# Linear attention with a learned feature map: the half-filled product of K, Q and V, for both branches in the two halves of TensorE's rows

## The chip, the cores and the metric

The kernel runs on one core of a Trainium2 chip, in one launch. The metric is the device time of that launch in microseconds. Five engines take part: TensorE (PE in the profile, PEld for its loads of stationary operands), VectorE (DVE), ScalarE (ACT), GpSimdE (POOL) and SyncE (SP), which issues nearly all transfers.

## The reference

Two attention branches, A and B, read the same input of 2048 tokens with 448 channels; each has 16 heads of 28 channels. A sigmoid gate mixes their outputs.

```
def _A_ref(x, wqkv, w_phi, wo):
    B, S, D = x.shape
    H = 16; Dh = D // H
    ...
    q, k, v = qkv[0], qkv[1], qkv[2]
    pq = jnp.einsum("bhsd,hdf->bhsf", q, w_phi)
    pk = jnp.einsum("bhsd,hdf->bhsf", k, w_phi)
    phi_q = jnp.concatenate([_softmax(pq, axis=-1), _softmax(-pq, axis=-1)], axis=-1)
    phi_k = jnp.concatenate([_softmax(pk, axis=-1), _softmax(-pk, axis=-1)], axis=-1)
    kv = jnp.einsum("bhsf,bhsd->bhfd", phi_k, v)
    z  = jnp.einsum("bhsf->bhf", phi_k)
    num = jnp.einsum("bhqf,bhfd->bhqd", phi_q, kv)
    den = jnp.einsum("bhqf,bhf->bhq", phi_q, z)[..., None] + 1e-6
    o = num / den
    return (lambda x, *d: x.transpose(*d))(o, 0, 2, 1, 3).reshape(B, S, D) @ wo
...
g = _sigmoid((x * gate_w).sum(-1, keepdims=True))
return g * a + (1 - g) * b
```

All data are float32.

## The kernel before, in words

**Tiles and products.** The 2048 tokens are 16 tiles of 128. For each tile TensorE makes K, Q and V of both branches (the learned map w_phi is folded into the weights of K and Q ahead, in fold). The matmuls take operands of the type fp32r; to come near float32, each factor is split into a high part and a low part (the rest), and three of the four products are made: high x high, high x low, low x high. The 448 channels are three and a half chunks of 128. The host appends the last 64 channels a second time, so that the fourth chunk has 128 rows: in x its rows 0 to 63 are the high part of these channels, and its rows 64 to 127 are overwritten with their low part (split_x), while the weights hold the same 64 rows twice. One matmul of the fourth chunk with the high weights thus makes two terms at once. With the low weights only its first 64 rows make a wanted term; the product of the low rows with the low weights comes along. The list XT (L414) names the 11 matmuls of a bank: four with the high weights, four with the low ones, and three with the low parts of x. The last of the second four, (3, 1, 3), is the half-filled one. mms (L416) issues them; k_proj, q_proj and v_proj call it once for each branch, with 432, 432 and 450 (branch 0, the gate's column among them) or 448 columns.

**PSUM banks.** K0 and K1 for K of the two branches, Q with two banks, VA and VB for V of the two branches, T0 for the sum over keys, O0 for a product of the last stage.

**What follows a product.** k_soft copies K out of its banks with ACT (pk) and makes its states, the two softmaxes, with reductions on DVE (L486, L487, L493), differences and products on POOL, exponentials on ACT; they lie in one of NE = 3 buffers (ret). v_out copies V with ACT into one of NV = 5 buffers (vs) and the gate's column into glog. q_front reduces Q on DVE (qmx, L520), subtracts into ru and sends it through DRAM (qd) to regroup it; q_soft reads it back and makes its softmaxes; DVE turns the result (L551). Results of tiles 0 to 7 are stored to DRAM (spill) and fetched again at the end. kv_acc (L497, matmuls at L505, T in the profile) adds two tiles' states times V into T0.

**The end.** num multiplies Q's states with the sums (N in the profile, L588, 32x32 tiles), DVE turns the bank (L599), POOL divides and gates, o_turn turns the result and splits it, and out_mm multiplies it with wo (O, 21 matmuls each tile, L636).

**Order.** The work of each step is given to a small planner (class Plan) with an engine, an estimated cost, and what it reads and writes. TensorE's steps run in the order in which steps() yields them; on each other engine the planner simulates the time and takes, of the steps that are ready, the one that is due first. The order that results is fixed at build time, and each engine runs it strictly in that order. The loop over p = 2 to 6 is a round of two tiles each: K of tile 2p, Q of tile 2p-2, kv_acc of 2p-2 and 2p-1, V of 2p+2, then K of 2p+1, Q of 2p-1, V of 2p+3. The inputs x of three pairs of tiles are held (NX = 3): load_x fetches, split_x converts with ACT and subtracts with POOL. In each round one or two chunks of wo are split too (ACT, POOL, and three transfers).

Of the kernel before, what the change touches and what calls it, by code (L numbers as in the profile page):

```python
# [13 lines left out]
P = 128  # L14
# [94 lines left out]
def steps():  # L109
# [5 lines left out]
    for p in range(2, 7):  # L115
        yield "x", p + 1
        yield "K", 2 * p
        yield "Q", 2 * p - 2
        if 2 * p - 2 < JIT:
            yield "S", 2 * p - 2, (JIT - 2 * p + 2) % 3 - 1  # L120
        yield "kv", 2 * p - 2, 2 * p - 1
        yield "wo", p - 2
        if p == 3:
            yield "wo", 6
        if p < 6:
            yield "V", 2 * p + 2
        yield "K", 2 * p + 1
        yield "Q", 2 * p - 1
        if 2 * p - 1 < JIT:
            yield "S", 2 * p - 1, (JIT - 2 * p + 1) % 3 - 1  # L130
        if p < 6:
            yield "V", 2 * p + 3
        if p == 6:
            yield "gates", 0, 12
            yield "gates_b", 0, 12
# [31 lines left out]
def hedgehog_mix(ctx: ExitStack, tc: tile.TileContext, xd, wv, wkt, wqt, wphi, wo, cmask, cpmask, out):  # L167
# [18 lines left out]
    rq = sb.tile([P, 2, 8 * FW], F32R, name="rq")  # L186
    rx = sb.tile([P, NX, 14 * P], F32R, name="rx")
    ret = sb.tile([P, 3 * 2048 + NE * 4 * D], F32, name="ret")
# [32 lines left out]
    wvh, wvl = (rv[:, i].rearrange("p (c n) -> p c n", c=4) for i in range(2))  # L221
    xs = [rx[:, i].rearrange("p (k t) -> p k t", k=7) for i in range(NX)]
    es = [re[:, i].rearrange("p (s n) -> p s n", s=2) for i in range(NE)]
# [15 lines left out]
    def free_v():  # L239
# [5 lines left out]
        mid["oT", 0], mid["oT", 1] = f[:, 6784:7168], ref[:, 4992:5376]  # L245
    hls = [rx[:, i].rearrange("p (s k t) -> p s k t", s=2, k=7) for i in range(NX)]
    obs = [ref[:, 4096 + D * i:4096 + D * i + D] for i in range(2)]
# [17 lines left out]
    def act(o, i, f=AF.Copy, **k):  # L265
        return lambda: A.activation(val(o), val(i), f, **k)  # L266
# [148 lines left out]

    def mms(t, w, name, k, lo, hi):  # L416
        x, o = xs[t // 2 % NX], t % 2 * P
        def go():
            for i, (xc, l, c) in enumerate(XT):
                nc.tensor.matmul(bank[name][:, k, lo:hi], x[:, xc, o:o + P], w[l][:, c], start=i == 0, stop=i == len(XT) - 1)  # L420
# [35 lines left out]

    def v_proj(t, b):
        w, n = v_weights(b)
        n_, k, kb = v_bank(t, b)
        add("PE", 11 * 0.203, mms(t, w, n_, k, 0, n),  # L460
            xkeys(t) + [("v" + h, c, b) for h in "hl" for c in range(4)], [kb])
# [8 lines left out]

    def k_proj(t, b):
        add("PE", 11 * 0.197, mms(t, feat((wkh, wkl), b), f"K{b}", 0, FO, FZ),
            xkeys(t) + wkeys("k", (b,)), [("K", b)])
# [36 lines left out]

    def q_proj(t, b):
        add("PE", 11 * 0.197, mms(t, feat((wqh, wql), b), "Q", b, FO, FZ),
            xkeys(t) + wkeys("q", (b,)), ["Q"])
# [186 lines left out]
    for what, *a in steps():  # L700
# [18 lines left out]
        elif what == "qf":  # L719
            q_front(*a)  # L720
        elif what == "Q":
            for b in range(2):
# [103 lines left out]
```

## Time and profile before

| | us |
|---|---|
| time, median of 3 runs | 338.06 (337.44 to 338.69) |
| the profiled execution's own time | 338.86 |
| its span, first to last instruction | 337.0 |
| PE busy | 329.7 |
| weight loads (PEld) busy | 295.5 |
| DVE busy | 280.6 |
| POOL busy | 250.8 |
| ACT busy | 145.2 |

Busy times are sums over the span; matmuls are pipelined, so that PE counts as busy also where it does not run at its peak. A matmul's record is longer than the distance to the next one's start: 359 ns on the average for Q, of which 352 take 72.1 us together. A row of a group of instructions has the line, the engine, the operation, the tiles written and read, the shapes, the count, the busy time and the mean duration in ns, and then the idle time of the engine before them with what ended it. A row of the timeline has start, length, engine, line, operation, tiles, shapes and count. The chain is followed back from the last instruction, at each step to what released it.

### The profile page before, as it was taken

To read this page: it belongs to the slowest core of one execution; us is meant where nothing else is said; L and a number is where in the kernel's file an instruction comes from. 1 tells how busy PE (TensorE), PEld (TensorE's weight loads), DVE (VectorE), ACT (ScalarE), POOL (GpSimd) and SP (SyncE) were. 2 spreads that over 40 slices of the span, in tenths; PEclk is the share of its full clock that TensorE was granted. 3 is DMA by queue.
4 is the path that set the end of the run, shared out by engine and by line. 5 is a ranking of instruction groups with operands and counts; after the bars stand their busy time and mean duration, and the time that the engine had idled before them with its cause. 6 is when DMAs were issued, how large, how long until landed. Compare 5 with 4: busy or idle time off the path is not lost.

```text
span 337.0 us, 8897 instructions
## 1 busy us (share of the span) xinstructions
PE 329.7 (98%) x3742; PEld 295.5 (88%) x3742; DVE 280.6 (83%) x339; ACT 145.2 (43%) x236; POOL 250.8 (74%) x210
## 2 busy tenths in 40 slices
PE   7999999999999999999999999999999999999994
PEld 6977899998999999999999999999788888788894
DVE  3648879699797896969899979797899999999960
ACT  3747944372365462624445344432052433523331
POOL 7018669999999969989896999694269768887400
PEclk9999999999999999999999999999999999999999
DMA  7773046531297757647646330765886355131011
GB/s 248 215 244 97 2 125 189 165 119 41 70 336 251 217 187 191 238 136 238 217 123 262 88 110 15 277 255 182 236 255 236 135 191 197 61 147 56 31 54 55
DMA packets 29871, 54.73 MB, mean 162 GB/s; under 512 B 4632, under 2 KB 25480, under 8 KB 27528
## 3 DMA queue, kind: packets, MB, share of 16 engines
q1 hardware_dynamic: 29576, 54.06, 48.7%
q8 instruction: 29, 0.48, 0.6%
q0 software_dynamic: 256, 0.12, 0.1%
q14 instruction: 10, 0.08, 0.1%
HBM read 31.54 MB, written 24.22 MB: 165 GB/s over the span
## 4 chain that ended last, share of the span: by engine, by line
PE 65%; DVE 18%; POOL 8%; DMA 4%; issue 3%; ACT 1%; SPq 1%; DVEq 0%; POOLq 0%; ACTq 0%
PE Q L420 15%; PE K L420 14%; PE O L636 10%; PE VA L420 8%; PE VB L420 8%; POOL ret L263 3%; PE T L505 3%; DVE rv L599 3%; POOL rv L608 3%; DVE ret L551 3%; PE N L588 2%; DMA ret<-in_wv 2%; DVE sm L493 2%; DVE rx L263 1%; DVE qsm L546 1%
## 5 line engine op out<-in xcount | busy, mean ns | idle before, releaser
L420 PE MATMUL Q<-rq,rx 128*128 128x432 f32 x352 | 72.1, 359 | 0.0
L420 PE MATMUL K<-rk,rx 128*128 128x432 f32 x352 | 71.8, 359 | 0.0
L636 PE MATMUL O<-rk,rx 128*128 128x448 f32 x336 | 70.6, 368 | 0.1
L636 PEld LDWEIGHTS O<-rk,rx 128*128 128x128 f32 x336 | 62.5, 188 | 8.5 <-ACT rx L627 1.2
L420 PEld LDWEIGHTS Q<-rq,rx 128*128 128x128 f32 x352 | 65.9, 188 | 3.8 <-DVE ru L263 0.4
L420 PEld LDWEIGHTS K<-rk,rx 128*128 128x128 f32 x352 | 66.1, 188 | 3.1
L266 ACT ACTIVATE ret<-ret 128x896 f32<-128x896 f32 x48 | 45.7, 951 | 46.3 <-POOL ret L263 45.3
L263 POOL TENSOR_TENSOR ret<-ret,sm 128x896 f32<-128x896 f32 x32 | 53.9, 1707 | 2.4 <-DVE sm L494 2.2
L493 DVE TENSOR_REDUCE sm<-ret 128x32 f32<-128x896 f32 x32 | 33.8, 1070 | 6.2 <-ACT ret L266 6.2
L551 DVE STREAM_TRANSPOSE ret<-ret 128x2048 f32<-128x2048 f32 x16 | 36.5, 2283 | 0.9 <-POOL ret L263 0.6
L263 POOL TENSOR_TENSOR ret<-pk,mx 128x896 f32<-128x896 f32 x16 | 27.3, 1707 | 11.6 <-DVE mx L486 11.6
L546 DVE TENSOR_REDUCE qsm<-ret 128x32 f32<-128x896 f32 x32 | 33.3, 1058 | 2.6 <-ACT ret L266 2.5
L420 PE MATMUL VA<-rv,rx 128*128 128x450 f32 x154 | 34.3, 370 | 0.0
L420 PE MATMUL VB<-rv,rx 128*128 128x448 f32 x154 | 33.9, 367 | 0.0
L263 POOL TENSOR_TENSOR ret<-qmn,ru 128x896 f32<-128x896 f32 x16 | 28.2, 1765 | 6.9 <-DVE ret L551 4.2
L266 ACT ACTIVATE ret<-ru 128x896 f32<-128x896 f32 x16 | 15.2, 951 | 42.1 <-issue 19.6
L420 PEld LDWEIGHTS VB<-rv,rx 128*128 128x128 f32 x154 | 28.6, 188 | 3.4 <-issue 0.8
L420 PEld LDWEIGHTS VA<-rv,rx 128*128 128x128 f32 x154 | 28.6, 189 | 2.9 <-ACT rk L266 0.4
L263 POOL TENSOR_TENSOR ret<-ret,qsm 128x896 f32<-128x896 f32 x16 | 27.3, 1705 | 0.9
L263 POOL TENSOR_TENSOR ret<-mx,pk 128x896 f32<-128x896 f32 x16 | 27.3, 1707 | 0.7 <-DVE mx L487 0.7
L540 DVE TENSOR_REDUCE qmn<-ru 128x32 f32<-128x896 f32 x16 | 17.0, 1062 | 10.6 <-DMA ru<-qd 10.5
L608 POOL TENSOR_TENSOR rv<-rv,rd 128x896 f32<-128x896 f32 x14 | 23.8, 1703 | 1.1
(92 smaller groups left out, 443.6 us busy)
## 6 DMA issues: line engine op xcount, KB each, us to landing
ed<-ret SPq DMA_DIRECT2D x8, 1024.0 KB
ret<-ed SPq DMA_DIRECT2D x8, 1024.0 KB
qd<-ru SPq DMA_DIRECT2D x64, 112.0 KB
ru<-qd SPq DMA_DIRECT2D x16, 448.0 KB
out<-ret SPq DMA_DIRECT2D x16, 224.0 KB
wod<-wst SPq DMA_DIRECT2D x14, 224.0 KB
rk<-wod SPq DMA_DIRECT2D x2, 1568.0 KB
xraw<-in_xt SPq DMA_DIRECT2D x5, 512.0 KB
```

Of the source, the lines that this page charges most:

```text
L263: return lambda: ENG[eng].tensor_tensor(val(o), val(a), val(b), op)
L266: return lambda: A.activation(val(o), val(i), f, **k)
L420: nc.tensor.matmul(bank[name][:, k, lo:hi], x[:, xc, o:o + P], w[l][:, c], start=i == 0, stop=i == len(XT) - 1)
L493: put("DVE", 2 * D, lambda s=s, e3=e3: V.tensor_reduce(sm[:, s], e3, AX.X, OP.add), [ke[s], *([("u", 0, 1)] if t == 15 else [])], [("sm", ...
L505: nc.tensor.matmul(kvp()[32 * r:32 * r + DH + 1, b, g], vs[t % NV][:, b, h // 2, h % 2], es[t % NE][:, :, hs:hs + DH], start=(t == 0 and b ...
L540: put("DVE", 2 * D, lambda: V.tensor_reduce(qmn, tq.rearrange("p c b g f -> p c (b g) f"), AX.X, OP.min), [kt, *late], [kn])
L546: put("DVE", 2 * D, lambda s=s, e3=e3: V.tensor_reduce(qsm[:, s], e3, AX.X, OP.add), [ke[s], *late], [("qsm", i, s)])
L551: add("DVE", 2.25, lambda: V.transpose(eTf[slot], eq.rearrange("p s a c f -> p (s a c f)")), ke, turned(slot))
L588: nc.tensor.matmul(bank["N"][32 * g:32 * g + 32, r, 2 * b * P:2 * b * P + 2 * P], kvt[32 * r:32 * r + 32, b, s, g], eTp[slots[0] // 2][32 ...
L599: add("DVE", 0.07 + 1.08 * nt, lambda: V.transpose(ctr().rearrange("p (r n) -> p r n", r=4), bank["N"][:, :, :2 * nt * P]), ["N"], [("ctr" ...
L608: put(eng, 2 * D, lambda: ENG[eng].tensor_tensor(mid["o", n % 3].rearrange("p (c a f) -> p a c f", c=4, a=8), ctv()[:, :, i, :, :DH], rd[: ...
L636: nc.tensor.matmul(bank[pb][:, 0, :D], a, w, start=i == 0, stop=i == len(terms) - 1)
```

## The change

The half-filled matmul is taken out of the projections of the loop: k10, q10 and v10 issue 10 matmuls for each branch instead of 11 and leave the bank's sum open. A new step, halves, makes the missing terms of a K tile, a Q tile and (for tiles 6 to 13) a V tile: for each, one matmul of rows 0 to 63 for branch 0 and one of rows 64 to 127 for branch 1, into different banks. For the second, rows 64 to 127 need the high part of the last 64 channels, so x gets an eighth chunk, whose upper rows ACT fills with a further copy. The two wp tiles move into the place of kvt to make room.

So that the three kinds can share one step, V's 10 matmuls are made in the half round before (tile 2p+2+i, after everything else of the half round), and halves stands behind K and Q. The states of K, the copies of V and Q's front come after halves. kv_acc moves from the first half of the round to the second, behind halves. V of odd tiles from 7 on takes the bank O0 instead of VA for branch 0. K and Q before tile 4 and 2 and after 13 and 11, V before 6 and after 13 keep their 11 matmuls. The planner is told 0.3 us and 0.1 us for each matmul of halves.

```diff
     for p in range(2, 7):
         yield "x", p + 1
-        yield "K", 2 * p
-        yield "Q", 2 * p - 2
-        if 2 * p - 2 < JIT:
-            yield "S", 2 * p - 2, (JIT - 2 * p + 2) % 3 - 1
-        yield "kv", 2 * p - 2, 2 * p - 1
-        yield "wo", p - 2
...
-        if p < 6:
-            yield "V", 2 * p + 2
-        yield "K", 2 * p + 1
-        yield "Q", 2 * p - 1
-        if 2 * p - 1 < JIT:
-            yield "S", 2 * p - 1, (JIT - 2 * p + 1) % 3 - 1
-        if p < 6:
-            yield "V", 2 * p + 3
+        for i in range(2):
+            k, q, v = 2 * p + i, 2 * p - 2 + i, 2 * p + 1 + i
+            yield "k10", k
+            yield "q10", q
+            v = v if 6 <= v < 14 else None
+            yield "halves", k, q, v
+            if i:
+                yield "kv", 2 * p - 2, 2 * p - 1
+            yield "ks", k
+            yield "qf", q
+            if v:
+                yield "vo", v, 0
+                yield "vo", v, 1
+            if q < JIT:
+                yield "S", q, (JIT - q) % 3 - 1
+            if i == 0:
+                yield "wo", p - 2
+                if p == 3:
+                    yield "wo", 6
+            if p < 6:
+                yield "v10", 2 * p + 2 + i
...
-    rx = sb.tile([P, NX, 14 * P], F32R, name="rx")
+    rx = sb.tile([P, NX, 16 * P], F32R, name="rx")
...
-    wp = sb.tile([P, 2, 4, HP], F32, name="wp")
-    wpd = sb.tile([P, 2, 4, HP], F32, name="wpd")
...
+    wp, wpd = kvt[:, 0], kvt[:, 1]
...
         put(high, 4 * (hi - lo), act(t[:, 0:4, :], r) if high == "ACT" else ...)
+        if p < 7:
+            put("ACT", hi - lo, act(t[64:P, 7, :], r[64:P, 3, :]), [*kr, *after], [("xd", n, i) for i in range(lo // P, hi // P)])
...
-    def mms(t, w, name, k, lo, hi):
+    def mms(t, w, name, k, lo, hi, part=False):
         x, o = xs[t // 2 % NX], t % 2 * P
+        terms = [a for a in XT if not part or a != (3, 1, 3)]
         def go():
-            for i, (xc, l, c) in enumerate(XT):
-                nc.tensor.matmul(bank[name][:, k, lo:hi], x[:, xc, o:o + P], w[l][:, c], start=i == 0, stop=i == len(XT) - 1)
+            for i, (xc, l, c) in enumerate(terms):
+                nc.tensor.matmul(bank[name][:, k, lo:hi], x[:, xc, o:o + P], w[l][:, c], start=i == 0, stop=i == len(terms) - 1 and not part)
         return go
+
+    def halves(k, q, v):
+        keys, banks_, go = [], [], []
+        for t, kind in ((v, "v"), (k, "k"), (q, "q")):
+            if t is not None:
+                x, o = xs[t // 2 % NX], t % 2 * P
...
+                for b in range(2):
...
+                    go.append((name, i, lo, n, x[64 * b:64 * b + 64, 7 if b else 3, o:o + P], w[64 * b:64 * b + 64, 3]))
+        def run():
+            for name, i, lo, n, a, w in go:
+                nc.tensor.matmul(bank[name][:, i, lo:lo + n], a, w, start=False, stop=True)
+        add("PE", 0.3 + 0.1 * len(go), run, keys, list(dict.fromkeys(banks_)))
...
     def v_bank(t, b):
-        return (f"K{b}", 0, ("K", b)) if t == 1 else (("VA", "VB")[b], 0, ("VA", "VB")[b])
+        n = "O0" if b == 0 and t >= 7 and t % 2 else ("VA", "VB")[b]
+        return (f"K{b}", 0, ("K", b)) if t == 1 else (n, 0, n)
```

More of the change, by code (lines that the diff above doesn't have):

```diff
@@ L116, in steps @@
         yield "x", p + 1
-        yield "K", 2 * p
-        yield "Q", 2 * p - 2
-        if 2 * p - 2 < JIT:
-            yield "S", 2 * p - 2, (JIT - 2 * p + 2) % 3 - 1
-        yield "kv", 2 * p - 2, 2 * p - 1
-        yield "wo", p - 2
-        if p == 3:
-            yield "wo", 6
-        if p < 6:
-            yield "V", 2 * p + 2
-        yield "K", 2 * p + 1
-        yield "Q", 2 * p - 1
-        if 2 * p - 1 < JIT:
-            yield "S", 2 * p - 1, (JIT - 2 * p + 1) % 3 - 1
-        if p < 6:
-            yield "V", 2 * p + 3
+        for i in range(2):
[19 more added lines that the diff above has]
+                yield "v10", 2 * p + 2 + i
         if p == 6:
@@ L221, in hedgehog_mix @@
     wvh, wvl = (rv[:, i].rearrange("p (c n) -> p c n", c=4) for i in range(2))
-    xs = [rx[:, i].rearrange("p (k t) -> p k t", k=7) for i in range(NX)]
+    xs = [rx[:, i].rearrange("p (k t) -> p k t", k=8) for i in range(NX)]
     es = [re[:, i].rearrange("p (s n) -> p s n", s=2) for i in range(NE)]
@@ L245, in free_v @@
         mid["oT", 0], mid["oT", 1] = f[:, 6784:7168], ref[:, 4992:5376]
-    hls = [rx[:, i].rearrange("p (s k t) -> p s k t", s=2, k=7) for i in range(NX)]
+    hls = [rx[:, i, :14 * P].rearrange("p (s k t) -> p s k t", s=2, k=7) for i in range(NX)]
     obs = [ref[:, 4096 + D * i:4096 + D * i + D] for i in range(2)]
@@ L455, in v_first, with v_proj @@
             v_out(t, b)
-    def v_proj(t, b):
+    def v_proj(t, b, part=False):
         w, n = v_weights(b)
         n_, k, kb = v_bank(t, b)
-        add("PE", 11 * 0.203, mms(t, w, n_, k, 0, n),
+        add("PE", (11 - part) * 0.203, mms(t, w, n_, k, 0, n, part),
             xkeys(t) + [("v" + h, c, b) for h in "hl" for c in range(4)], [kb])
@@ L469, in v_out, with k_proj @@
             add("ACT", 0.2, act(glog[:, t:t + 1], lambda: bank[n_][:, k, D:D + 1], AF.Exp, scale=-1.0), [kb], [("gl", t)], ahead=9.0 * (t < 2))
-    def k_proj(t, b):
-        add("PE", 11 * 0.197, mms(t, feat((wkh, wkl), b), f"K{b}", 0, FO, FZ),
+    def k_proj(t, b, part=False):
+        add("PE", (11 - part) * 0.197, mms(t, feat((wkh, wkl), b), f"K{b}", 0, FO, FZ, part),
             xkeys(t) + wkeys("k", (b,)), [("K", b)])
@@ L509, in kv_acc, with q_proj @@
             [k for t in ts for k in (("e", t % NE, 0), ("e", t % NE, 1), ("v", t % NV, 0), ("v", t % NV, 1))], ["T0"])
-    def q_proj(t, b):
-        add("PE", 11 * 0.197, mms(t, feat((wqh, wql), b), "Q", b, FO, FZ),
+    def q_proj(t, b, part=False):
+        add("PE", (11 - part) * 0.197, mms(t, feat((wqh, wql), b), "Q", b, FO, FZ, part),
             xkeys(t) + wkeys("q", (b,)), ["Q"])
@@ L720, in hedgehog_mix @@
             q_front(*a)
+        elif what in ("k10", "q10", "v10"):
+            for b in range(2):
+                {"k": k_proj, "q": q_proj, "v": v_proj}[what[0]](*a, b, True)
+        elif what == "halves":
+            halves(*a)
         elif what == "Q":
```

12 lines of the change are left out of this document (added).

## The prediction, made before the changed kernel had run

> **What bounds the kernel now.** I read the page's busy line first, then the chain that ended last in order of time, then the windows, then single stretches of the timeline.
>
> ```profile
> span 337.0 us, 8897 instructions
> PE 329.7 (98%) x3742; PEld 295.5 (88%) x3742; DVE 280.6 (83%) x339; ACT 145.2 (43%) x236; POOL 250.8 (74%) x210
> ```
>
> A busy PE alone proves little, so the chain decides. From it, parts of the rounds p=2 to 6 of the loop, the first products behind it and the last stretch of the kernel (columns: start, length, what; a round is K, Q, T, V, K, Q, V):
>
> ```profile
> 79.74 0.99 PE T L505 x64
> ...
> 98.52 4.32 PE K L420 x22
> 102.84 4.31 PE Q L420 x22
> 107.14 1.71 PE T L505 x128
> 108.85 2.45 PE VA L420 x11
> 111.31 2.23 PE VB L420 x11
> ...
> 122.16 2.26 PE VA L420 x11
> ...
> 135.28 1.71 PE T L505 x128
> ...
> 152.55 2.23 PE VB L420 x11
> ...
> 191.54 1.71 PE T L505 x128
> 193.25 4.50 PE K L420 x22
> 197.74 4.30 PE Q L420 x22
> 202.05 4.32 PE K L420 x22
> ...
> 291.83 0.61 ACT rx L266
> 292.48 8.83 PE O L636 x42
> ```
>
> Each piece begins where the last one ends: between 79.7 and 236 us nothing but TensorE is on the chain, and a round costs 135.28 - 107.14 = 28.14 us. T is kv_acc (L505), so T at 79.74 is the second half of tiles 2 and 3, T at 191.54 tiles 10 and 11. The one stall of PE in the loop:
>
> ```profile
> PE T L505 <- POOL ret L263: 0.7, 1, 0.7
> ```
>
> The other engines are close behind. The windows (columns: length, then PE, PEld, DVE, ACT, POOL busy):
>
> ```profile
> 79.70:107.14 27.44, 27.40 (x200) 25.66 (x204) 23.01 (x27) 12.44 (x20) 26.84 (x20) 1.00 0.59 197
> 163.40:191.54 28.14, 28.14 (x266) 26.39 (x268) 27.80 (x34) 13.29 (x20) 23.77 (x19) 1.00 0.49 163
> 236.48:292.48 56.00, 55.87 (x959) 45.99 (x958) 54.04 (x62) 19.26 (x33) 39.64 (x39) 1.00 0.58 190
> ```
>
> POOL has 0.6 us free in the first, DVE 0.3 in the second and 2 in the third, where at 292.48 an output product waits for ACT, behind DVE. So a saving on PE counts only as far as POOL and DVE follow. The granted clock is 1.00 throughout.
>
> **The change part by part.**
>
> *The half-filled term.* From the chain one matmul of K or Q is 4.32/22 = 0.196 us, one of V 2.26/11 = 0.205 (branch 0) or 2.23/11 = 0.203. In the loop 10 K, 10 Q and 8 V tiles (6 to 13) each lose one full matmul per branch: 56 in all, 40 x 0.196 + 16 x 0.204 = 11.1 us. In their place stand 28 pairs of 64-row matmuls. Whether a pair runs at once no row of before shows directly; the nearest is N, whose row groups and banks are used in the same way, with 32-row tiles:
>
> ```profile
> L420 PE MATMUL Q<-rq,rx 128*128 128x432 f32 x352 | 72.1, 359 | 0.0
> L588 PE MATMUL N<-ret,kvt 32*32 32x256 f32 x1024 | 22.1, 385 | 0.0
> L588 PEld LDWEIGHTS N<-ret,kvt 32*32 32x32 f32 x1024 | 14.4, 103 | 6.2 <-issue 1.8 <-DVE qsm L546 0.3 <-DVE rv L625 0.3
> ```
>
> N's records overlap 1024 x 0.385 / 22.1 = 17.8 deep, against 352 x 0.359 / 72.1 = 1.75 for Q, which is only pipelining: 10.2 times as deep on 16 tiles. Loads overlap 1024 x 0.103 / 14.4 = 7.3 deep. So row tiles do run at once. Bounds for a pair: 0.199 us (one stream, perfect) and, at N's 10.2/16 = 64%, 0.199 / 0.64 = 0.31. I take 0.199, since the pair has Q's shape (128 columns, one load and one long stream) and N another (two instructions for each product, short loads). 28 pairs: 5.6 us.
>
> *Switching the array.* V after T takes 2.45 against 2.26, K 4.50 against 4.32: 0.19 us to come back from tiled to full. On the way in, the weight loads pause:
>
> ```profile
> 135.21 1.63 PEld L505 LDWEIGHTS T<-ret,vs 128*29 128x29 f32 x128 [0.29 <-issue]
> ```
>
> The last Q matmul streams 0.2 of that 0.29, so 0.09 us is drain, and a first load of 128 columns then stands uncovered, as on the way back. I charge 0.19-0.2 for each way. In the first half of a round (5 times) the halves stand between full products: 0.39. In the second half (5 times) kv_acc follows, whose own switches existed: 0.2 more. Together 2.95 us. The page "TensorEngine Tiling (Array Packing)" of the Trainium skill, section "Tiling Modes", says that changing the tiling mode drains TensorE; the 0.09 us agree. Saved: 11.1 - 5.6 - 2.95 = **2.6 us**.
>
> *kv_acc half a round later.* The 0.7 us stall at 79.7 was kv_acc of tiles 2, 3 waiting for POOL. It now stands behind V6, K5, Q3 and the halves, some 13 us later: the stall goes, **-0.7**. What is late next: tile 5's states, written behind this kv_acc; they need ACT, DVE and POOL first, longer than its 1.71 us.
>
> *Banks handed over later.* All of K, Q and V is now complete only after the halves, so the copies out of the banks come in a burst. In the first half of a round VB must be empty again 10 matmuls later, 2.05 + 0.2 us; K's banks 4.3 us later. Before, each had over 8 us. The copies now:
>
> ```profile
> 157.08 0.53 ACT L266 ACTIVATE vs<-VB 128x448 f32<-128x448 f32 x1
> 187.33 0.55 ACT L266 ACTIVATE pk<-K 128x448 f32<-128x448 f32 x1 [0.84 <-PE K L420]
> 187.07 4.47 PE L420 MATMUL Q<-rq,rx 128*128 128x432 f32 x22
> ```
>
> A prompt copy starts 187.33 - 187.07 = 0.26 us after the last matmul and takes 0.55: free after 0.8, no stall. A late one (VB complete at 154.78, copy ended at 157.61) takes 2.83: 0.6 us of stall. There are 3 such tight places (V 7, 9, 11). Bounds 0 and 3 x 0.6 = 1.8; I take one late copy in two rounds, **+0.3**.
>
> *Round p=6 has no V behind the halves.* K of tile 13 follows at once and must wait for ACT to empty K of tile 12: 0.26 + 0.55, less 0.09 of drain that is counted: **+0.7** (up to 0.95 more if an exponential of 0.95 us has just begun). What is queued behind it: Q of tile 11, which needs the Q bank 0.7 + 0.2 + 3.9 = 4.8 us after the halves. DVE's rows for tile 10:
>
> ```profile
> 192.24 1.08 DVE L520 TENSOR_REDUCE qmx<-Q 128x32 f32<-128x896 f32 x1
> 193.36 1.15 DVE L263 TENSOR_TENSOR ru<-Q,qmx 128x448 f32<-128x448 f32 x2
> 207.61 3.37 POOL L263 TENSOR_TENSOR ret<-ret,sm 128x896 f32<-128x896 f32 x2
> 208.10 1.09 DVE L263 TENSOR_TENSOR ru<-Q,qmx 128x448 f32<-128x448 f32 x2
> ```
>
> Tile 10's bank was empty 194.51 - 191.54 = 3.0 us after Q: nothing. Tile 11's took 209.19 - 202.05 = 7.1, which would cost 2.3; I take 0, as tile 10 is the one in question.
>
> *kv_acc of tiles 12 and 13.* K of 13 ended at 197.74 and POOL finished its states at 210.98: 13.2 us. Now kv_acc of 10, 11 (1.8), K14 (4.5), V14 (2.25) and K15 (4.3) lie between: 12.9. **+0.3** (0 to 2).
>
> *The copies of x.* Five more ACT copies of 64x256 and two of 64x128 ahead of the loop, a quarter of the 1.05 us conversion beside them at most, on an engine that is 43% busy and issues no transfers: 0. If ACT were full they would lengthen it by 1.5 us. The raw buffer, and with it SP's next load, is freed 0.3 us later at worst, a round ahead of use. wp in kvt's place costs nothing: one is dead before the other lives. Of what is moved, only two parts issue transfers, all on SP: q_front (four stores each) and q_soft (one load, for tiles 0 to 7 also a store of 1 MB) come behind the halves, a microsecond at most after their old place, with more than a round until the result is fetched; wo's split (one load, two stores) stays in the first half. POOL issues none in the loop.
>
> *Sum:* -2.6 - 0.7 + 0.3 + 0.7 + 0 + 0.3 = **-2.0 us** where PE reaches N. Does the end follow? DVE's rows there:
>
> ```profile
> 236.52 1.09 DVE L520 TENSOR_REDUCE qmx<-Q 128x32 f32<-128x896 f32 x1 [1.18 <-PE Q L420]
> 239.21 2.32 DVE L599 STREAM_TRANSPOSE rv<-N 128x2048 f32<-128x2048 f32 x1 [0.41 <-PE N L588]
> ```
>
> DVE waits 1.18 + 0.41 = 1.6 us for PE, so 1.6 pass by themselves; of the other 0.4 I take 0.2: **-1.8 us**, 0.5%. The profiled execution took 338.86 us, 1.86 beside its span of 337.0; it would come to 337.1. It lies 0.8 above the median of the runs shown, and from that median the forecast is 338.06 - 1.8 = **336.3 us**. About 0.5% (1.7 us) is what a measurement of this kernel can tell from no change.
>
> **The rivals.**
>
> *Pairs one after the other* (the change doesn't do what it says): 28 x 0.199 = 5.6 us back, +3.8: 341.9, slower. N's depth speaks against it; N is another type of product.
>
> *Pairs overlap only as well as N's tiles:* 0.31 a pair, +3.1: 339.4, no change. The page "TensorE: Matmul & The Clock Gate" of the Trainium skill, section "Measured speedup vs the span model", gives 3.07x for four row tiles and 10.6x for sixteen tiles; the trace's 10.2 agrees with the latter. By 3.07/4 an estimate for a pair would be 0.26 us, and the sum about 0.
>
> *The banks become the wait:* ACT runs in order, and its exponentials wait for POOL:
>
> ```profile
> ACT ret L266 <- POOL ret L263: 38.9, 28, 6.5
> ```
>
> A VB copy queued behind one stalls PE, and POOL is 98% busy at 79-107. At the longest wait, 6.5 us, each of the three tight places costs 6.5 + 0.55 - 2.25 = 4.8: up to 14 us. It decides from 3.5 us in all. With 2 us at each, +4.2: 342.3, slower. Against it: VB's copy is now the one that PE needs first, and the order is planned by that.
>
> *DVE holds the end:* 54.04 of 56.00 us; if the states come to DVE so late that it reaches N no earlier, all is lost: 338.1.
>
> *Everything hides:* without the 1.3 us of stalls that I charged, and with the end following in full, -3.3: 334.8. For it: PE's own waits in the loop are 0.7 us in all so far.
>
> **How the numbers follow.** The forecast 0.50, of which 0.28 beyond -1.7 us and 0.22 within; everything hides 0.10; pairs as N 0.08; DVE holds 0.10, banks in a small measure 0.04; banks outright 0.10; pairs in turn 0.08. So faster 0.38, same 0.44, slower 0.18. The likeliest case's own range is 335.2 to 337.5. Holding eight in ten takes in the bounds of pairs and banks in part: 334.3 to 340.5.
>
> **What would show it.** Right: records of 64x128 in pairs that start within some 0.01 us, three starts 0.2 apart in each halves step; 0.2 us before and behind; no stall of T on POOL at 79 us; rounds of 27.5 us; a PE wait of 0.7 us on ACT (pk) ahead of K13. Wrong: starts of the second of a pair 0.2 us after the first; PE waiting for ACT vs<-VB in each first half; T of 12, 13 waiting on POOL by over 1 us; N earlier but the product of 292.48 not.

## The result, and the profile after

The changed kernel took 342.51 us (median; 342.27 to 342.71) against 337.98 of the kernel before on the same chip: a ratio of 1.0133, interval 1.0112 to 1.0153. It is 4.5 us slower, where 1.8 us faster was forecast. The profiled execution took 342.37 us, and its page begins:

```profile
span 340.6 us, 8911 instructions
PE 330.4 (97%) x3742; PEld 290.9 (85%) x3742; DVE 284.6 (84%) x339; ACT 147.7 (43%) x244; POOL 250.7 (74%) x210
PEclk9999999999999999999999979999999999999999
PE 34%; DVE 26%; POOL 20%; DMA 8%; issue 5%; ACT 4%; SPq 1%; DVEq 0%; POOLq 0%; ACTq 0%
```

The instructions of PE are as many as before and its busy time has grown by 0.7 us, though the pairs should have taken some off. PE has only 34% of the chain that ended last (65% before); DVE and POOL have 46%. In one slice of 40 the granted clock falls, which happens nowhere before.

The pairs do what the change says. From the timeline of the changed kernel (start, length, engine, line, operation), the halves step of a half round:

```profile
106.63 0.47 PE L452 MATMUL O<-rv,rx 64*128 64x450 f32 x1
106.63 0.47 PE L452 MATMUL VB<-rv,rx 64*128 64x448 f32 x1
106.94 0.37 PE L452 MATMUL K<-rk,rx 64*128 64x432 f32 x2
107.13 0.37 PE L452 MATMUL Q<-rq,rx 64*128 64x432 f32 x2
```

The two matmuls of V start at the same time. The pair of K stands 0.31 us behind them, the pair of Q 0.19 us behind that of K, and the next product, at 107.43, 0.30 us behind Q. From the first start to the next product that is 0.80 us, as much as the 3 x 0.199 and the 0.2 for the way back that were charged. In the windows (length, then PE, PEld, DVE, ACT, POOL busy, granted clock, DMA share, GB/s), the first stretch is a round of the loop, the second is p=6 up to kv_acc of tiles 10 and 11:

```profile
92.74:120.39 27.65, 27.65 (x262) 25.03 (x261) 24.76 (x29) 12.97 (x22) 24.92 (x18) 1.00 0.65 212
175.64:204.00 28.36, 25.21 (x242) 22.37 (x240) 24.39 (x27) 12.10 (x20) 23.56 (x18) 0.94 0.39 123
```

A round takes 27.65 us, 0.49 less than before. The second stretch has no V, and yet takes longer than a round: PE idles for 3.15 us of it, at a mean clock of 0.94. The waits of PE (on what, sum, count, longest) say for whom:

```profile
PE Q L427 <- DVE ru L267: 3.4, 2, 2.4
PE K L427 <- ACT pk L270: 1.4, 2, 0.8
```

The 0.7 us for POOL's states is gone; 4.8 us for DVE and ACT stand in its place, in two spots. The first lies ahead of the loop. ACT's timeline there, and PE's:

```profile
49.47 0.41 ACT L270 ACTIVATE rx<-xraw 64x256 fp32r<-64x256 f32 x1 [5.46 <-DMA xraw<-in_xt]
49.91 0.54 ACT L270 ACTIVATE pk<-K 128x448 f32<-128x448 f32 x1
```

```profile
50.50 4.59 PE L427 MATMUL K<-rk,rx 128*128 128x432 f32 x22 [0.60 <-ACT pk L270]
56.12 4.59 PE L427 MATMUL Q<-rq,rx 128*128 128x432 f32 x22 [1.02 <-DVE ru L267]
```

The row at 49.47 is one of the new copies, 0.41 us long. It stood at the head of ACT's queue for 5.46 us until its transfer had landed, and the copies out of K's bank and the exponentials behind it waited with it. In the kernel before, the same spot of ACT's queue holds such copies and exponentials, and each waits for PE or POOL only:

```profile
45.90 0.55 ACT L266 ACTIVATE pk<-K 128x448 f32<-128x448 f32 x1 [1.61 <-PE K L420]
47.87 0.95 ACT L266 ACTIVATE ret<-ret 128x896 f32<-128x896 f32 x1 [1.43 <-POOL ret L263]
```

The second spot is p=6. PE and DVE of the changed kernel (Q11, K13 and the like are in short the products of that tile):

```profile
185.46 4.11 PE L427 MATMUL Q<-rq,rx 128*128 128x432 f32 x20
...
190.00 0.37 PE L452 MATMUL Q<-rq,rx 64*128 64x432 f32 x2
191.16 4.19 PE L427 MATMUL K<-rk,rx 128*128 128x432 f32 x20 [0.79 <-ACT pk L270]
197.72 5.75 PE L427 MATMUL Q<-rq,rx 128*128 128x432 f32 x20 [2.36 <-DVE ru L267]
```

```profile
188.21 1.09 DVE L526 TENSOR_REDUCE sm<-ret 128x32 f32<-128x896 f32 x1 [2.93 <-ACT ret L270]
...
193.19 2.30 DVE L584 STREAM_TRANSPOSE ret<-ret 128x2048 f32<-128x2048 f32 x1
...
196.51 1.16 DVE L267 TENSOR_TENSOR ru<-Q,qmx 128x448 f32<-128x448 f32 x2
```

Q of tile 11 waits until DVE has emptied the bank of tile 10, whose last products ended at 190.37. DVE works on almost without a break, but on four reductions, two reciprocals and a turn that stand ahead of qmx in its queue; the first of these had itself waited 2.93 us for ACT. The bank is free at 197.67, 7.3 us after Q. Then comes something else: the same 20 matmuls of Q that take 4.11 us at 185.46 take 5.75 here, since the granted clock is down:

```profile
197.72:203.40 5.68, 5.68 (x22) 5.06 (x22) 5.00 (x7) 1.90 (x2) 4.59 (x4) 0.70 0.54 148
```

0.30 x 5.68 = 1.7 us are lost to it. Finer windows of the same trace give a clock of 1.00 during the pause, of 0.92 in the first 0.68 us behind it, of 0.50 from 198.4 to 201.4 us and of 0.74 in the next 0.6: in all about 3.4 us at half the clock. The account is closed by the rows of kv_acc and N of both kernels, after first:

```profile
67.19 1.78 PE L538 MATMUL T<-ret,vs 128*29 128x56 f32 x128
...
240.29 2.75 PE L621 MATMUL N<-ret,kvt 32*32 32x256 f32 x128
```

```profile
65.29 1.78 PE L505 MATMUL T<-ret,vs 128*29 128x56 f32 x128
...
236.41 2.76 PE L588 MATMUL N<-ret,kvt 32*32 32x256 f32 x128
```

Up to the first kv_acc (tiles 0, 1) 1.90 us are lost. From there to N it is 173.10 against 171.12, 1.98 more: waits of 0.79 + 2.36 and 1.7 of clock are +4.85, so the pairs and the stall that went gave, by subtraction, about -2.9 (forecast: -2.6 - 0.7). From N to the end it is 340.6 - 240.29 = 100.3 against 337.0 - 236.41 = 100.6. So the span grew by 1.90 + 1.98 - 0.3 = 3.6 us. The rest of the 4.5 is that before's profiled execution lay 0.9 us above its median.

### The profile page after: what moved, and what is told of

Read it like the earlier page. It is cut to its first block, busy times and chain, and to the rows that moved or that the text cites. A ratio compares the mean times of both kernels' runs of the same rounds, so it can differ in the third digit from the quotient of the medians.

```text
span 340.6 us, 8911 instructions
## 1 busy us (share of the span) xinstructions
PE 330.4 (97%) x3742; PEld 290.9 (85%) x3742; DVE 284.6 (84%) x339; ACT 147.7 (43%) x244; POOL 250.7 (74%) x210
## 4 chain that ended last, share of the span: by engine, by line
PE 34%; DVE 26%; POOL 20%; DMA 8%; issue 5%; ACT 4%; SPq 1%; DVEq 0%; POOLq 0%; ACTq 0%
POOL ret L267 14%; PE O L669 10%; DVE ret L584 6%; PE Q L427 6%; PE K L427 5%; DMA qd<-ru 5%; DMA ru<-qd 3%; DVE ru L267 3%; POOL rv L641 3%; PE VB L427 3%; DVE qmx L553 3%; DVE rv L632 3%; ACT ret L270 2%; DVE qsm L579 2%; PE VA L427 2%
## 5 line engine op out<-in xcount | busy, mean ns | idle before, releaser
L427 PE MATMUL Q<-rq,rx 128*128 128x432 f32 x332 | 70.3, 367 | 3.6 <-DVE ru L267 3.4
L427 PEld LDWEIGHTS Q<-rq,rx 128*128 128x128 f32 x332 | 63.3, 192 | 8.2 <-DVE ru L267 4.5
L427 PE MATMUL K<-rk,rx 128*128 128x432 f32 x332 | 68.3, 360 | 1.4 <-ACT pk L270 1.4
L427 PEld LDWEIGHTS K<-rk,rx 128*128 128x128 f32 x332 | 62.0, 188 | 5.4 <-ACT pk L270 2.1
L427 PE MATMUL VB<-rv,rx 128*128 128x448 f32 x146 | 32.3, 367 | 0.0
L427 PEld LDWEIGHTS VB<-rv,rx 128*128 128x128 f32 x146 | 27.1, 188 | 3.4 <-issue 0.8
L621 PE MATMUL N<-ret,kvt 32*32 32x256 f32 x1024 | 22.1, 385 | 0.0
L427 PE MATMUL VA<-rv,rx 128*128 128x450 f32 x95 | 21.4, 372 | 0.0
L553 DVE TENSOR_REDUCE qmx<-Q 128x32 f32<-128x896 f32 x16 | 17.2, 1074 | 4.6 <-PE Q L427 3.2
```

The source lines that it names most:

```text
L553: put("DVE", 2 * D, lambda: V.tensor_reduce(mx, p4(), AX.X, OP.max), ["Q"], [km])
L621: nc.tensor.matmul(bank["N"][32 * g:32 * g + 32, r, 2 * b * P:2 * b * P + 2 * P], kvt[32 * r:32 * r + 32, b, s, g], eTp[slots[0] // 2][32 ...
```

## The experiments

Theory A: the pairs gain what was forecast, and the loss comes from two places, the copies in ACT's queue and p=6. Rival B: the time saved on PE can't reach the end in any order, because states and DVE don't follow.

**The copies alone (e1).** The kernel before, with x's eighth chunk, the copies that fill it and wp in kvt's place, and nothing else of the change:

```diff
+        if p < 7:
+            put("ACT", hi - lo, act(t[64:P, 7, :], r[64:P, 3, :]), [*kr, *after], [("xd", n, i) for i in range(lo // P, hi // P)])
```

> The kernel before, with one edit: ACT also makes the copies of x's last 64 channels (five of 64x256, and 64x128 ones ahead of them) that the change needs; nobody reads them. The order of all other engines is that of before. Theory A (the new copy of 64x256 stands in ACT's queue ahead of the copies of K of tile 1 and waits there for its transfer, 5.5 us in the changed kernel, and PE stalls behind full banks): slower by 1.5 to 2 us, some 339.8, with PE waits on ACT pk and on DVE ru near 50 and 56 us of 0.6 and 1.0 us. Theory B (the changed kernel is late there because its moved states load DVE and POOL otherwise): the same as before within 0.3 us, since neither is touched. As predicted (copies cost nothing): the same as before.

Measured: 340.53 us against 338.11, ratio 1.0071 [1.0043, 1.0099]. Its first kv_acc and N:

```profile
66.68 1.78 PE L506 MATMUL T<-ret,vs 128*29 128x56 f32 x128
...
237.87 2.75 PE L589 MATMUL N<-ret,kvt 32*32 32x256 f32 x128
```

In ACT's queue the copy of 64x256 starts at 48.96 us, after 4.84 us of waiting for its transfer. PE's new wait is 1.0 us, of Q for DVE (ru); the one for pk that was expected beside it isn't there. Against the profiled execution of before, copies of less than half a microsecond cost 1.4 us ahead of the loop, and N is 1.5 us later; the medians lie 2.4 us apart. That the copies alone make the kernel slower, as theory A had it, is shown.

**The copies behind the conversion (e2).** The changed kernel, where the copy may start only after the conversion of the same columns:

```diff
-            put("ACT", hi - lo, act(...), [*kr, *after], ...)
+            put("ACT", hi - lo, act(...), [*kr, *after, *h], ...)
```

> The changed kernel, with one edit: each copy of x's last channels also waits for the conversion of the same x, so that it stands behind it in ACT's queue and not ahead of K's copies. Theory A: K of tile 4 starts at 69.3 to 69.5 us instead of 71.2, and the time falls by 1.7 to 2 us to about 340.6, if the wait of Q of tile 11 on DVE stays as it is; up to 1 us less if DVE is then just as late there. Theory B (DVE and POOL set the time, whatever PE does): under 0.5 us gained, the wait of Q of tile 11 growing by what is saved ahead of it.

341.64 us, 1.0078 [1.0039, 1.0117], so less was gained than the 1.7 to 2 us of theory A. The waits ahead of the loop are gone, but ACT's order, planned anew, brings others: VB waits 1.4 us in all for the copies of V, and K13 1.29 us for pk instead of 0.79. Q11 waits 2.36 us as it did.

How much the copies cost ahead of the loop differs from execution to execution. In seventeen traces of the changed kernel and its variants, the first kv_acc starts at 66.36 to 68.08 us where the copies stand ahead of the conversion (five of them, 67.2 on the average) and at 64.48 to 66.61 where they stand behind it (twelve, 65.5): 1.7 us between the averages.

**Whole rows in place of pairs (e3).** The changed kernel, with halves made of the old matmuls on all 128 rows:

```diff
-                    go.append((name, i, lo, n, x[64 * b:64 * b + 64, 7 if b else 3, o:o + P], w[64 * b:64 * b + 64, 3]))
+                    go.append((name, i, lo, n, x[:, 3, o:o + P], w[:, 3]))
```

> The changed kernel, with one edit: the halves step keeps its place and all orders stay, but each of its matmuls takes all 128 rows (the full half-empty product of before). This is the price of the pairs alone. Theory A (pairs run at once and cost two switches of 0.2 us): a round of the loop grows from 27.6 to 28.2 us (12 full matmuls of 0.2 in place of 6 pairs and their switches; 6 x 0.2 = 1.2 us more, about 0.6 us of switches less), and the end follows by 0 to 2.6 us, since the Q11 wait on DVE may shrink by what PE is later. Theory C (the halves cost as much as they save): a round stays at 27.6.

343.14 us, 1.0141 [1.0096, 1.0186]: not to be told from the changed kernel by its time, but the trace tells them apart. kv_acc in the rounds:

```profile
92.91 1.78 PE L538 MATMUL T<-ret,vs 128*29 128x56 f32 x128
121.09 1.78 PE L538 MATMUL T<-ret,vs 128*29 128x56 f32 x128
```

A round is 28.18 us, against 27.65 with pairs and 28.14 before: the pairs, switches included, are worth 0.53 us a round. Had the pairs run only as well as N's tiles, or one after the other, nothing would have been saved: the 12 matmuls of 0.2 us are 2.4 us, six pairs of 0.31 us with the 0.6 us charged for switches are as much, and pairs in turn are more.

**p=6: work put into the wait (e5).** The changed kernel, with V of tile 14, branch 0, taken from behind K14 to between K13 and Q11:

```diff
+            if q == 11:
+                yield "V", 14, 0
```

> The changed kernel, with one edit: the first branch of V of tile 14 (11 matmuls, 2.25 us) stands between K of tile 13 and Q of tile 11 in the round p=6, instead of behind K of tile 14. Every queue is the same up to there. Theory A (PE idles there 2.4 us for DVE to empty the Q bank, and the clock drop that follows costs another 1.6): the wait falls from 2.4 to under 0.4 us, the 20 matmuls of Q11 take 3.95 us instead of 5.75, and N comes 3.5 to 4 us earlier, less what kv_acc of tiles 12 and 13 then waits for POOL (0 to 2 us): 338.5 to 341. Theory B: kv_acc of 12 and 13 or N waits for what was saved; 342 or more.

346.2 us, 1.0233 [1.0188, 1.0279]: the time is that of theory B (342 or more). Q11 no longer waits, but K14 waits 4.08 us for ACT (pk), and VB and K13 wait 0.85 and 1.30 us ahead of it.

**p=6: PE kept busy (e10).** Eleven more matmuls, whose result nobody reads, behind K13, with the queues of all other engines as in the changed kernel:

```diff
+        if (t, b) == (13, 1):
+            go = lambda go=go: (go(), mms(12, v_weights(0)[0], "VA", 0, 0, D + 2)())
```

> The changed kernel, with one edit: behind K of tile 13, ahead of Q of tile 11, PE makes 11 more matmuls (2.25 us) into the bank VA, which is empty there; nobody reads them. All queues of all other engines are those of the changed kernel. Theory A1 (the 1.8 us by which the 20 matmuls of Q11 are too long are a drop of PE's clock that follows its idle 2.4 us): Q11 still begins when DVE has emptied the bank, the PE wait is under 0.3 us, its 20 matmuls take 3.95 us instead of 5.75, no clock under 1 in that slice, and kv_acc of tiles 10 and 11 starts 1.5 to 1.8 us earlier; the time falls by 1 to 1.8 us, to about 341. Rival (the length is a second wait of Q's second branch for its bank): no change.

```profile
174.81 1.78 PE L541 MATMUL T<-ret,vs 128*29 128x56 f32 x128
...
196.40 4.22 PE L427 MATMUL Q<-rq,rx 128*128 128x432 f32 x20
...
201.13 1.78 PE L541 MATMUL T<-ret,vs 128*29 128x56 f32 x128
...
216.18 0.99 PE L541 MATMUL T<-ret,vs 128*29 128x56 f32 x64 [1.24 <-POOL ret L267]
```

With 2.4 us of useless work in place of the wait, the 20 matmuls of Q take 4.22 us again instead of 5.75, and the stretch 26.32 us instead of 28.35: the pause of PE brought the clock down. The mean granted clocks of all executions agree: 0.999 to 1.000 in the four here, 0.992 to 0.995 in the four of the changed kernel. But of the 2.0 us gained at kv_acc of tiles 10, 11, that of tiles 12, 13 loses 1.24 to a new wait for POOL's states, and from the first kv_acc to N the kernel needs 238.88 - 66.36 = 172.52 us against 173.10: 0.6 us are left. This execution, the fastest of four, took 341.26 us, the median 343.02 (1.0132 [1.007, 1.0194]). So the time is not lower than that of the changed kernel; what the other three lost was not traced.

**p=6 as before (e8), and with the copies behind the conversion too (e9, "repaired").**

```diff
+        if p == 6:
+            yield "K", 12
+            yield "Q", 10
+            yield "kv", 10, 11
+            yield "wo", 4
+            yield "K", 13
+            yield "Q", 11
+        for i in range(2 * (p < 6)):
```

> The changed kernel, with one edit: the round p=6 is that of before (K12, Q10, kv_acc 10 and 11, K13, Q11 whole, V of tile 13 whole in the round before); the rounds 2 to 5 keep the halves. Theory A (the burst of copies with no V behind it is what costs 4.8 us at p=6): no PE wait on pk or ru at p=6, N 4 us earlier than in the changed kernel, near 336.3, and the time 4 to 4.8 us less, 338 to 338.5. Theory B (DVE and POOL are late there in any order): PE waits of over 2 us in all between 175 and 240 us, 340.5 or more.

> As the kernel with the round p=6 of before, and each copy of x's last channels also stands behind the conversion of the same x. Theory A: the two losses add up and are both gone: 336.5 to 337.5, faster than before by 0.3 to 0.5%; four rounds with pairs save 0.55 each and the 0.7 us wait on POOL. Theory B: the time saved comes back as a wait of V's bank for ACT (0.9 us was seen there once) or as a later N: 338.5 or more.

e8: 341.05 us, 1.0076 [1.005, 1.0103], well above theory A's number: the waits at p=6 and the lowered clock are gone, those ahead of the loop (1.03 and 1.00) stay, and kv_acc of tiles 10, 11 now waits 1.13 us for POOL. From the first kv_acc to N e8 needs 171.89 us, only 1.2 less than the changed kernel, though 4.85 us of waits and lowered clock are gone and only some 0.5 us is given up with the pairs of that round. e9: 339.33 us against 337.97, with a ratio of 1.0005 [0.9974, 1.0036] (the ratios are as recorded, and need not be the quotient of two medians); theory B had said 338.5 or more. Together the repairs bring back what was lost, but not the gain of the pairs. A second look at e9 (e9b: 338.74, 1.0004 [0.9979, 1.0029]) shows what PE waits for now:

> The kernel with both repairs (the round p=6 of before, and the copies behind the conversion) once more, as the base for the next three on the same chip. It was 339.3 against 338.0 in its first comparison; with four rounds of pairs it has saved 2.7 us by kv_acc of tiles 10 and 11 in its trace, and was level at N. Expected again: 338 to 339.5, kv_acc of tiles 10 and 11 waiting 0.5 to 1 us for POOL.

```profile
66.61 1.78 PE L544 MATMUL T<-ret,vs 128*29 128x56 f32 x128
...
175.06 1.78 PE L544 MATMUL T<-ret,vs 128*29 128x56 f32 x128
...
191.97 0.99 PE L544 MATMUL T<-ret,vs 128*29 128x56 f32 x64 [0.91 <-POOL ret L273]
...
238.01 2.75 PE L627 MATMUL N<-ret,kvt 32*32 32x256 f32 x128 [1.35 <-issue]
```

```profile
236.09 1.09 DVE L579 TENSOR_REDUCE qmn<-ru 128x32 f32<-128x896 f32 x1 [2.74 <-DMA ru<-qd]
237.09 0.76 DVE L614 STREAM_TRANSPOSE kvt<-kvs 128x256 f32<-128x256 f32 x2
```

kv_acc of tiles 10, 11 waits 0.91 us for POOL, and N 1.35 us for kvt, the turned sums, which stand in DVE's queue behind a minimum that waits 2.74 us for a transfer.

**The order of before for V, pairs for K and Q alone (e7).** Copies behind the conversion, V of 11 matmuls with two banks, halves for K and Q only.

> The order of before (V whole behind each half round, kv_acc in the first half), but the last products of K and Q stand behind Q as pairs, and V keeps its 11 matmuls; the copies of x's last channels stand behind the conversion. K's and Q's states start when these pairs are done. In the first half kv_acc follows (4 matmuls of 0.196 less, 2 pairs and one switch more: 0.2 us saved), in the second V follows (two switches: nothing saved). Theory A: rounds of 27.95 us, the 0.7 us wait on POOL stays, K12's and Q10's banks are emptied behind kv_acc without a PE wait: 337 to 337.8. Theory B (DVE and POOL set the time): 338 to 339.5, as K's states come 4.3 us later.

342.43 us, 1.0103 [1.0036, 1.0169], slower than both theories had it. kv_acc of tiles 12, 13 waits for POOL, and runs at a lower clock behind that (64 matmuls in 1.56 us, 0.99 before the wait):

```profile
213.36 0.99 PE L533 MATMUL T<-ret,vs 128*29 128x56 f32 x64
216.60 1.56 PE L533 MATMUL T<-ret,vs 128*29 128x56 f32 x64 [2.25 <-POOL ret L262]
```

**Is the saved time on the path at all? Repaired with whole rows (e12); kv_acc later (e11).** e12 is e9 with e3's edit; all queues are the same. In e11 kv_acc of tiles 10, 11 moves behind K13; there it reads the states of tile 13 in place of tile 10's, since the two share a buffer, so it waits for those (16 us) and answers nothing.

> The repaired kernel, with one edit: halves on all 128 rows in place of the pairs, all queues the same. Theory A (PE sets the time, the pairs are worth 0.55 us a round): slower than the repaired kernel by 2.2 us, N 2.2 us later. Theory B (near the loop's end the states, made by DVE, ACT and POOL, set the time, and PE waits for what it has saved): slower by 0 to 0.7 us; the waits for POOL at kv_acc of 10 to 13 shrink by 1 us or more, and N comes under 1 us later.

> The repaired kernel, with one edit: kv_acc of tiles 10 and 11 stands behind K of tile 13 in the round p=6, 4.3 us later in PE's order, so that the states of tile 11 have 20 us instead of 16; the planner orders ACT, DVE and POOL anew from there. Theory A: the wait of 0.9 us goes and N comes 0.9 us earlier, 0.5 to 1 us faster than the repaired kernel. Theory B: kv_acc of 12 and 13 or N waits for it instead, the time stays.

e12: 338.56 us, 1.0011 [0.9984, 1.0037], the same as e9b on the same chip, where theory A had 2.2 us more. Its rows:

```profile
65.81 1.78 PE L544 MATMUL T<-ret,vs 128*29 128x56 f32 x128
...
176.28 1.78 PE L544 MATMUL T<-ret,vs 128*29 128x56 f32 x128
...
236.24 2.75 PE L627 MATMUL N<-ret,kvt 32*32 32x256 f32 x128
```

From the first kv_acc to that of tiles 8, 9 it needs 110.47 us; e9b needs 175.06 - 66.61 = 108.45. So pairs save 2.0 us up to there. From the first kv_acc to N it is 170.43 against 171.40: all of it is gone and 1.0 us more, and neither of e9b's two waits is in e12, whose PE waits for nothing on this stretch. Here rival B holds: saved time turns into waiting. The sizes are those of one execution: e9b's profiled one took 340.07 us, 1.3 above its median, and e9's 340.04, 0.7 above; that whole rows and pairs end level is what the medians say too. (e11: 355.66, 1.0517.) The question left was which of the two waits takes it.

**DVE's order and POOL's work, one at a time and crossed.** e13 (also f3) is e9 with less work on POOL: the big part of the subtraction in split_x runs on 16 of 256 columns for pairs 5 to 7, so that low parts are left out there. e14 (f2) is e9 with kvt ahead of the waiting minimum on DVE. e15 (f4) has both; f1 is e9. f1 to f4 ran on one chip.

```diff
+        m = 16 if p >= 5 else hi - lo
...
-        put("DVE", 2 * D, lambda: V.tensor_reduce(qmn, ...), [kt, *late], [kn])
+        put("DVE", 2 * D, lambda: V.tensor_reduce(qmn, ...), [kt, *late, *([("kvt", 0), ("kvt", 1)] if k == 12 else [])], [kn])
```

> The repaired kernel, with one edit: POOL's largest subtraction for x is made on 16 of 256 columns for the pairs of tiles 5 to 7 (the rest of x's low parts is left out there and stays that of an earlier pair); all queues the same. It takes 1.6 us from POOL three times. Theory B with POOL as the engine: no wait of kv_acc for POOL, N 1 to 2 us earlier, 1 to 2 us faster. Theory A: the same as the repaired kernel, except for the 0.9 us of kv_acc of 10 and 11. If DVE or the transfers are what is late: kv_acc earlier, N not.

> The repaired kernel (e9) with one change of order on VectorE: the turn of kv_acc's last state (kvt) stands ahead of the query-side minimum of tile 12, which waits for a transfer. All other queues are the same. Theory A (N waits 1.1 to 1.5 us because kvt stands behind a minimum that waits 2.8 us for its transfer): N's wait goes, N starts 1.0 to 1.4 us earlier, and the time is 337.3 to 338. Rival B (the end belongs to VectorE's work, which only changes its order): N starts earlier, but the time stays at 338.5 to 339.

> The same order on VectorE on top of the repaired kernel with less work on POOL (the subtraction of the big parts on 16 of 256 columns for pairs 5 to 7; the low parts are left out there). Theory A: no wait for states and none for kvt is left, N starts 1.0 to 1.4 us earlier than with less work on POOL alone, the time is 336 to 337. Rival B: 338 to 338.5, as with less work on POOL alone.

> Two edits crossed, all four kernels on one chip: the repaired kernel as it is (this run), with kvt ahead of the waiting minimum on VectorE, with less work on POOL, and with both. Theory A (both the order on VectorE and POOL's states hold the end, each behind the other): this one 338.5 to 339, each edit alone 0.3 to 1 us below it, both together 2 to 2.5 us below it. Rival B (the pairs' saving can't reach the end at all): all four within 0.5 us.

> kvt ahead of the waiting minimum. Theory A: 337.5 to 338.2, no wait of N for kvt, a wait of T for POOL's states stays. B: 338.5 to 339.

> Less work on POOL for pairs 5 to 7 (subtraction on 16 of 256 columns, the low parts left out). Theory A: 337.7 to 338.5, N still waits 1.1 us. B: 338.5 to 339.

> Both edits. Theory A: 336 to 336.7, neither wait. B: 338 to 339.

| | first time (two chips) | on one chip (before: 337.79) |
|---|---|---|
| repaired | 338.74, 1.0004 [0.9979, 1.0029] | 337.95, 1.0005 [0.9976, 1.0034] |
| kvt first | 337.28, 0.999 [0.9965, 1.0014] | 337.69, 0.9989 [0.9964, 1.0014] |
| less on POOL | 338.24, 0.998 [0.9954, 1.0007] | 336.55, 0.9951 [0.9932, 0.9971] |
| both | 336.14, 0.9943 [0.9923, 0.9962] | 335.82, 0.9938 [0.9915, 0.9961] |

Less work on POOL (e13): kv_acc no longer waits for POOL, and N still waits 1.10 us.

```profile
234.46 2.75 PE L628 MATMUL N<-ret,kvt 32*32 32x256 f32 x128 [1.10 <-issue]
```

Kvt first (f2), PE's and DVE's rows: N no longer waits, and the wait for POOL stays, as in e9b.

```profile
64.66 1.78 PE L544 MATMUL T<-ret,vs 128*29 128x56 f32 x128
...
190.01 0.99 PE L544 MATMUL T<-ret,vs 128*29 128x56 f32 x64 [0.92 <-POOL ret L273]
...
234.67 2.76 PE L627 MATMUL N<-ret,kvt 32*32 32x256 f32 x128
```

```profile
231.94 1.67 DVE L616 TENSOR_SCALAR kvt<-kvt 128x4 f32<-128x4 f32 x2
233.84 1.08 DVE L579 TENSOR_REDUCE qmn<-ru 128x32 f32<-128x896 f32 x1 [0.23 <-DMA ru<-qd]
```

Both (f4): no wait of either kind is left.

```profile
64.48 1.78 PE L545 MATMUL T<-ret,vs 128*29 128x56 f32 x128
...
232.84 2.76 PE L628 MATMUL N<-ret,kvt 32*32 32x256 f32 x128
```

From the first kv_acc to N: 171.40 (e9b), 170.01 (f2), 169.54 (e13), 168.36 (f4; 169.14 in e15); before, 171.12. f4 thus shows the 2.0 us of the pairs and the 0.7 of the stall at N, and from there to the end needs 333.1 - 232.84 = 100.3 us like the changed kernel. On one chip kvt first gives 0.3 us, less POOL 1.4, both 2.1, as theory A had it (2 to 2.5) with the larger share on POOL; the two single edits were expected at 0.3 to 1. The intervals of repaired and kvt first overlap, and so do those of less POOL and both, so what the order of kvt is worth is shown by the traces only. f4 leaves out work and is no kernel to use. The best complete version, kvt first, is level with the kernel before; no complete version that ran is faster than it. Whether less work on POOL would help whole rows as much was not run, so f4's gain in time isn't shown to be the pairs' alone; up to N e12's PE has no wait that it could take away.

So each theory holds in part. The pairs gain what was forecast, and the two places cost what A says; but up to N the gain turns into waits for POOL and DVE, as B says, until both are relieved.

One more thing spreads the times. f1's profiled execution took 341.11 us, 3.2 above its median. PE and ACT in it:

```profile
181.55 4.06 PE L433 MATMUL VB<-rv,rx 128*128 128x448 f32 x11 [2.34 <-ACT vs L276]
```

```profile
180.12 0.95 ACT L276 ACTIVATE ret<-ru 128x896 f32<-128x896 f32 x1 [5.57 <-DMA ru<-qd]
180.97 0.53 ACT L276 ACTIVATE vs<-VB 128x448 f32<-128x448 f32 x1
```

An exponential that waits for a late transfer holds the copy out of VB behind it, PE pauses, and the 11 matmuls take 4.06 us at the lowered clock. The same happened in e14's profiled execution (340.48 us), where VB waits 2.44 us; f2's, of the same kernel as e14, has no such wait. The slack of over 8 us that the copies of V had before is no longer there.

## Why the prediction was wrong, by its own steps

**The pairs: right.** Forecast 0.199 us a pair and 2.6 in all; a step of three pairs takes 0.80 us with one switch, as charged, and e3 and e12 show 0.53 a round and 2.0 up to tile 9. The starts are not all 0.2 apart, as forecast: the first gap is 0.31, the second 0.19. The rivals of pairs in turn, or as N's tiles, are out.

**The stall at 79 us: right.** -0.7, and no T waits in the changed kernel. kv_acc of tiles 12, 13 (+0.3) did not wait there either; in e7 (2.25) and e10 (1.24) it did.

**K13 at p=6: right.** +0.7 forecast, 0.79 measured.

**Q11's bank: wrong, 0 taken, 2.36 measured.** The prediction had the price: "Tile 11's took 7.1, which would cost 2.3". It chose tile 10's 3.0 us "as tile 10 is the one in question", as if the time to empty a bank belonged to the tile. It belongs to what stands ahead in DVE's queue, and the planner made that queue anew: the bank took 7.3 us. The other end of the bound would have been nearly exact. How much of this is the new order and how much that DVE had lost 2.93 us waiting for ACT just before, no run separates.

**What the pause costs besides: missing.** 1.7 us of lowered clock behind it, which no row of before shows, as its longest wait in the loop was 0.7.

**The copies of x: wrong, 0 taken, 1.4 us by e1 and 1.9 in the changed kernel.** The step weighed the copies as work, "on an engine that is 43% busy". Their length was indeed nothing, though they are eight (four of 64x256, four of 64x128) and the larger take 0.41 us, more than a quarter of 1.05; that one of them waits for a transfer at the head of an in-order queue, ahead of copies that PE needs, was the cost. The prediction knew that ACT runs in order, and reckoned with it for VB's copies in a rival; for the added copies it asked only how long they are.

**VB's copies: 0.3 for late ones.** None in the profiled execution; waits of 0.3 to 2.4 us in executions of variants (e2, e5, e8, e11, e14, f1). The rival "banks become the wait", with 342.3 us, comes nearest, but at Q's bank and by DVE, not at VB's by ACT; it had a chance of 0.10.

**"Does the end follow?": in part.** N to the end is as long as before, so it does follow N. But the saving must first reach N, and with both losses repaired it did not (e9, e12): kv_acc of tiles 10, 11 then waits for POOL and N for kvt. The step counted the states of tiles 12, 13 and DVE behind N; those of 10, 11 and kvt's place ahead of N were not asked about. So even without the two losses the time would have been about that of before, not 1.8 us below it.

In numbers: -2.0 was forecast at N in the profile's time; add 1.9 (copies), 2.36 (bank), 1.7 (clock): +4.0, and +3.88 was measured. That it fits so closely is partly luck: 0.6 us charged for stalls that did not come stand against 0.4 that the pairs and the stall gave less. Nor can the terms be had back one by one: without the lowered clock N came only 0.6 us earlier (e10), and without the waits for ACT and DVE at p=6 1.2 (e8), as other waits took their place.

## What to carry to other kernels

An instruction added to an in-order engine is priced by what it waits for and by who stands behind it, not by its length and the engine's share of busy time. Where a change has the queues planned anew, the time in which a bank is emptied is no property of the tile: take the bad end of the bound, unless the row shows what stands ahead in the new order. And time saved on one engine counts only as far as the engines that feed its next step keep up. An experiment tells whether they do: take the saving away, leave all queues as they are, and see whether the time grows.

## What the hardware showed unexpectedly

A pause of TensorE of 2.3 us can cost 1.7 us again. Behind waits of 2.36 us (after), 2.34 (f1), 2.44 (e14) and 2.25 (e7) the next matmuls run slow (20 in 5.75 us instead of 4.11; 11 in 4.06 and 4.01 instead of 2.38, f2's; 64 in 1.56 instead of 0.99), and without the pause they do not (e10). After waits of 1.0 to 1.48 us (e1, e9, e9b) nothing of the kind is seen; no wait in the loop lies between 1.48 and 2.25, so where the change comes is open. In the changed kernel the clock stands at half for about 3.4 us, from 0.6 us behind the end of the pause on, which makes the 1.7 us. The page "TensorE: Matmul & The Clock Gate" of the Trainium skill says, in the section "What's actually happening", that an idle TensorE is granted half its clock, and sets it by windows of 3.4 us; the 3.4 us at half agree with such a window. Its section "HAM oscillation — how this bites in real kernels" asks only that no gap be longer than about 3.4 us; here 2.25 us were enough.
